# Sixteen pieces of weights on the GpSimd queue: one transformer stack on one core

## The chip, the cores and the metric

The kernel runs on one core of a Trainium2 chip. The core has a tensor engine (PE, with its weight loads listed apart as PEld), a vector engine (DVE), a scalar engine (ACT), GpSimd (POOL) and a sync engine (SP). Each runs its own instruction stream in order; they meet through semaphores. DMA transfers are issued from SP, ACT or POOL and are moved by 16 DMA engines. The metric is device time in microseconds (us), the median of the runs shown; lower is better.

## The reference

The input x has 2048 tokens of 448 features, in bf16. Four layers follow each other, each with a layer norm and a residual sum:

```
x = x + A(layernorm(x))      # layer 0
x = x + B(layernorm(x))      # layer 1
x = x + A(layernorm(x))      # layer 2, the same weights
x = x + B(layernorm(x))      # layer 3, the same weights

A: q, k, v = x @ wqkv, 16 heads of 28
   each token attends to 8 keys: itself and 2, 4, ... 14 tokens back (masked before the start)
   softmax, weighted sum of v, then @ wo (448 x 448)
B: (x @ w_gate) * (x @ w_up) @ w_down      # 448 -> 1792 -> 448, no activation
```

## The kernel before, in words

**Layout.** Even and odd tokens are split, so that a dilation of two becomes neighbouring tokens. x stays on the chip in 16 blocks of 128 tokens (`x_sb`). The layers are cut into chunks of 256 or 512 tokens; a job such as A01 is chunk 1 of layer 0, B10 chunk 0 of layer 1. `SEQ` lists the order of the jobs, so that attention chunks and GLU chunks of neighbouring layers overlap.

**Layer norm** (`ln_chunk`, lines 722 to 770). DVE computes statistics (L732, L734), ACT the reciprocal root (L735, L737), DVE the normed block `xn_sb` (L753). Blocks of layer 0 are transposed on PE against an identity (L763) and copied back by ACT or DVE (L769); later ones by a DMA transpose on SP.

**Attention.** `qk_chunk` (L823) multiplies the transposed block by WQK, accumulating over four row pieces (all matmuls of this kind have line L511, a helper). WQK is not loaded as it is: the raw rows come in four "stage" pieces into the space of `hT`, and eight copies (L675; ACT, DVE or POOL) spread each head's 28 columns over 32. Four spare columns per head carry part of V through eight more copies (L683), which wait until the first two QK chunks are done. Scores are L967, their exponential L974, the mask product L984, the weighted sum L1004, the norm L1029 to L1042, the output projection again L511, the residual sum L1059.

**GLU** (`b_chunk`, L1069). Fourteen units per chunk; each streams the chunk past gate and up weights (WGU, L511), ACT copies the gate (L1095), DVE multiplies into `hT` (L1098). The down projection WD follows (L511; for the last blocks L1110, with L1114).

**What sets the order.** A planner inside the program (`Sched`) plays all engines forward with estimated durations and landing times, and at each moment gives a free engine the ready operation with the lowest priority number. Its result is written out as fixed instruction streams. The priorities come from the job (`JP`), the kind of operation (`PR`, added by the first part of the operation's key) and the call. A transfer's key counts too: the x loads have the kind "x", so `PR['x']` moves them. The stage pieces have no entry. Estimated landings (`XL`, `STL`, `WVL`, `BL`, `WOL`) and `LINE_T`, the estimated time of a block of PE instructions, only steer the planner.

**Transfers before.** SP issues, in this order: the two halves of the first x chunk, stage pieces 1 and 3, x chunk 1, two V weight pieces, two small stage pieces, x chunks 2 and 3, four wo pieces, two WD pieces, two up pieces (L601 in the profile, the helper `plain_dma`). ACT issues stage pieces 0 and 2 first, and the two gate pieces later, held back by `tmin` (`KT`). After them SP issues the ones (L690) and the transfers that carry V (L864, L875). POOL issues none; it builds masks, constants and some copies. Before the first real matmul PE runs a fill of 96 matmuls on zeros (L666).

Of the kernel before, what the change touches and what calls it, by code (L numbers as in the profile page):

```python
# [9 lines left out]
S = 2048  # L10
D = 448
H = 16
DH = 28
F = 1792
# [3 lines left out]
NCH = S // 512  # L18
# [6 lines left out]
FC = F // 128  # L25
# [5 lines left out]
MAXALT = 2  # L31
PE_T = ("00", "01", "02", "03", "04")
HEAD_LN = 5
HEAD_P = (-381.43, -49.67, 14.22, 69.7, -45.56)
HOLD_A = 1000.0
HOLD_BA = 2000.0
HOLD_BB = 500.0
HOLD_N = 2
S_EST = 288.0
AV_EST = 288.0  # L40
# [6 lines left out]
VT = 4  # L47
# [5 lines left out]
AVC = True  # L53
AVC_E = ("act", "dve")
NBK = 8
PR = {'AV': -30.61, 'rstd': 31.29, 'bn': -4.6, 'N': -44.12, 'Gps': 146.17, 'Tps': -150.33, 'H': -24.74, 'S': 182.09, 'VT': 39.93, 'Ex': 74.94, 'G': 97.99, 'xn': -34.8, 'QK': 6.58, 'Ddps': -216.87, 'V': 10.56, 'x': -0.57, 'lnv': -319.88, 'Oc': 120.77, 'Oa': -56.11, 'R': 196.58, 'VVps': -26.27, 'Yps': -14.03, 'PW': 266.54, 'T': -7.3, 'mv': -7.38, 'Rs': 73.61, 'Rl': 145.28, 'QKps': -19.32, 'E': -12.39, 'wqk': -11.84, 'wqp': -232.02}
JP = {'A20': 55.19, 'B32': 45.24, 'B34': -59.99, 'A22': 64.41, 'B13': -156.92, 'A21': 25.01, 'B12': -69.87, 'A02': -34.56, 'A03': -34.8, 'B30': 7.81, 'B31': 37.42, 'B10': -123.7, 'B11': -163.2, 'A23': 119.73, 'A04': -39.52, 'B33': -120.76, 'A01': -46.54, 'B14': -1.29, 'A00': -55.83}
XL = (2300.0, 2200.0, 4200.0, 5000.0, 5500.0)
WVL = 5000.0
STL = (2400.0, 2600.0, 2900.0, 2800.0)  # L60
VONES_L = 18000.0
BL = (11000.0, 15000.0, 8000.0)
KT = (13000.0, 13500.0)
WOL = 6000.0
PAIR_PLAIN = (7, 7)
ACH = {0: (256, 512, 512, 512, 256), 2: (512, 512, 512, 512)}
BCH = {1: (256, 512, 512, 512, 256), 3: (256, 512, 512, 512, 256)}
# [1 line left out]
FILL = 30  # L69
SEED = 190  # L70
JITTER = 0
ATT_P = 1.96
A_CAP = 6
B_CAP = 6
SEQ = "A00 A01 B10 A02 B11 A03 A04 B12 A20 B13 A21 B14 B30 A22 B31 A23 B32 B33 B34".split()
# [58 lines left out]
class Sched:  # L134
# [8 lines left out]
    QUEUE = 64  # L143
    REFILL = 256.0
    LINE = 256
    LINE_T = 3800.0

    def __init__(self):
        self.ops = []
# [5 lines left out]
    def add(self, engs, ins, est, deps=(), prio=0.0, mode=None, acquire=None, release=(), dma=None, lat=0.0, after=None, selfd=(), tmin=None, alt=()):  # L155
        if isinstance(engs, str):
            engs = (engs,)
        if not isinstance(est, dict):
            est = {e: float(est) for e in engs}
        op = Op(engs=engs, ins=ins, est=est, deps=[d for d in deps if d is not None], mode=mode, prio=prio,  # L160
                acquire=acquire, release=release, idx=len(self.ops), dma=dma, lat=lat, after=after, selfd=set(selfd), tmin=tmin, alt=alt)
        op.deps += list(selfd)
        op.prio += JITTER * self.rng.random()
        for _, k in ins:
            k = k[0] if isinstance(k, list) and k else k
            if isinstance(k, tuple) and k[0] in PR and k[0] != "cross":
                op.prio += PR[k[0]]
                break
        self.ops.append(op)
        for n, (fn, keys) in enumerate(ins):  # L170
            for k in (keys if isinstance(keys, list) else [keys]):
                if k is not None:
                    assert k not in self.ready, k
                    self.ready[k] = (op, n)
        return op
# [364 lines left out]
def build(nc, A_x, A_wqkv, A_wo, B_w_gate, B_w_up, B_w_down, out):  # L540
# [16 lines left out]
    mv = sb([128, NBLK, 2], dt.float32, "mv")  # L557
    lnv = sb([128, NBLK], dt.float32, "lnv")
    rstd = sb([128, NBLK], dt.float32, "rstd")
# [6 lines left out]
    WGU = sb([128, 7, F], bf, "WGU")  # L566
    WD = sb([128, FC, D], bf, "WD")
# [15 lines left out]
    sc = Sched()  # L583
    LAST = sc
    sem_names = ["pe", "act", "dve", "pool"]
    sem_names += [f"d_x{i}" for i in range(NCH)] + ["d_stg0", "d_stg1", "d_stg2", "d_stg3", "d_wv", "d_wo", "d_wg0", "d_wg1", "d_wu0", "d_wu1", "d_wd0", "d_wd1", "d_out", "d_out2"]
    sem_names += ["d_x0h"]
    sem_names += [f"d_t{li}_{j}" for li in range(4) for j in range(len(CH[li]))]
    sem_names += [f"d_p{li}_{j}" for li in (0, 2) for j in range(len(CH[li]))] + [f"d_v{q}" for q in range(NQB)] + ["d_one", "d_stv"]
    vt_all = nc.dram_tensor("vt", (256, S), bf, kind="Internal").ap()  # L590
# [9 lines left out]
    def plain_dma(q, dst, src, key, sem, deps=(), lat=3000.0, prio=0.0, tmin=None):  # L600
        sc.add(q, one(lambda E: E.dma_start(dst, src), key), {"sp": 520.0, "act": 500.0, "pool": 1000.0}[q], deps=deps, dma=sem, mode=0, lat=lat, prio=prio, tmin=tmin)  # L601

    CH_ROWS = [0, 128, 192, 320]
    stage = hT[:].rearrange("p f s n -> p (f s n)")
# [10 lines left out]
        r = v.ap[0][0]  # L615
        return bass.AP(tensor=v.tensor, offset=v.offset, ap=[[r, 128], [128 * r, 2], [1, hi - lo]])

    for c in (1, 3, 0, 2):
        plain_dma("act" if c % 2 == 0 else "sp", stage[:, 2 * D * c:2 * D * (c + 1)], A_wqkv[CH_ROWS[c]:CH_ROWS[c] + 128, 0:2 * D], ("stg", c), f"d_stg{c}", lat=STL[c], prio=-60 if c % 2 == 0 else -49.9)
    load_x(1)  # L620
    for a in range(2):
        plain_dma("sp", WV[:, 2 * a:2 * a + 2, :], wv_rows(a, 2 * D, 3 * D), ("wv", a), "d_wv", lat=WVL, prio=-48.9)
# [65 lines left out]
    ones_dst = vt_all.rearrange("(t e) (a n) -> t e a n", e=32, n=128)[:, DH:32]  # L688
    ones_src = ones32[0:32, :].unsqueeze(1).to_broadcast([32, 16, 128])
    plain_dma("sp", ones_dst, ones_src, ("vones",), "d_one", deps=["c_ones"], lat=VONES_L, prio=-40)  # L690
    for j in range(4):
        dst = wo_g[32 * j:32 * j + DH, :, :]
        src = A_wo.rearrange("(c j e) d -> j e c d", c=4, j=4, e=DH)[j]
        plain_dma("sp", dst, src, ("wo", j), "d_wo", deps=["c_wo"], lat=WOL, prio=-45)
    for n in range(2):
        f0, f1 = F // 2 * n, F // 2 * (n + 1)
        plain_dma("sp", WGU[64:128, :, f0:f1], B_w_up[:, f0:f1].rearrange("(k p) f -> p k f", p=64), ("wu", n), f"d_wu{n}", lat=BL[1], prio=-43.5)
        plain_dma("act", WGU[0:64, :, f0:f1], B_w_gate[:, f0:f1].rearrange("(k p) f -> p k f", p=64), ("wg", n), f"d_wg{n}", lat=BL[0], tmin=KT[n], prio=-90)
    for n in range(2):
        plain_dma("sp", WD[:, 7 * n:7 * n + 7, :], B_w_down[F // 2 * n:F // 2 * n + F // 2, :].rearrange("(c p) e -> p c e", p=128), ("wd", n), f"d_wd{n}", lat=BL[2], prio=-44)  # L700
    WDR = [("wd", 0), ("wd", 1)]
    WO = [("wo", j) for j in range(4)]

    rings = {n: [None] * k for n, k in (("xn", NXN), ("o", NO), ("v", NV), ("v2", NV2), ("e", NE if PAIRED else 2 * NE), ("r", NR), ("g", NG))}
# [364 lines left out]
    def b_chunk(li, j, n_b, prio):  # L1069
# [4 lines left out]
        nt, b0 = t1 - t0, t0 // 128  # L1074
        tdeps = [("T", li, B) for B in range(b0, t1 // 128)]

        def unit(fc):
            acq = Banks(2, kind=1)
            def out(which):
                return ps[:, acq[which], 0:nt]  # L1080
            return dict(bk=acq, out=out, n=nt, deps=[(w, n) for w in ("wg", "wu") for n in range(2)],
                        keys=(("Gps", li, j, fc), ("Ups", li, j, fc)), fc=fc)

        us = [unit(fc) for fc in range(FC)]
        for m in range(FC):
# [6 lines left out]
            for u in us[m:m + 1]:  # L1092
                bk, fc = u["bk"], u["fc"]
                gs, prev = ring("g", ("H", li, j, fc))
                sc.add("act", one(lambda E, gs=gs, bk=bk: E.activation(g_sb[:, gs, 0:nt], ps[:, bk[0], 0:nt], ACT.Copy), ("G", li, j, fc)), act_est(nt),  # L1095
                       deps=[("Gps", li, j, fc), prev], release=[(bk, 0)], prio=prio)
                war = hslot_users.get((hs, "prev"), WQKR + [f"c_mk{k}" for k in range(3)])
                sc.add("dve", one(lambda E, gs=gs, bk=bk, fc=fc: E.tensor_tensor(hT[:, fc, hs, 0:nt], g_sb[:, gs, 0:nt], ps[:, bk[1], 0:nt], ALU.mult), ("H", li, j, fc)), dve_est(nt),  # L1098
                       deps=[("G", li, j, fc), ("Ups", li, j, fc)] + war, release=[(bk, 1)], prio=prio)
# [3 lines left out]
        for B in range(t1 // 128 - 2, t1 // 128) if last else ():  # L1103
            i = B - b0
            halves = ((0, D),) if B % 2 == 0 else ((0, D // 2), (D // 2, D))
            for c0_, c1_ in halves:
                bk = Banks(1, kind=1)
                ins = []
                for fc in range(FC):
# [5 lines left out]
                       deps=[("Dd", li, B, c0_), ("x", li - 1, B), ("xn", li, B)], release=[(bk, 0)], prio=prio)  # L1115
                r, b = divmod(B, 8)
                plain_dma("act" if c0_ == 0 and len(halves) > 1 else "sp", out_par[r][:, b, c0_:c1_], x_sb[:, B, c0_:c1_], ("out", B, c0_), "d_out2" if c0_ == 0 and len(halves) > 1 else "d_out", deps=[("x", li, B, c0_)], lat=2500.0, prio=prio)
        for i in range(0, nt // 128 - 2 * last, 2):
            B = b0 + i
            bk = Banks(2, kind=1)  # L1120
# [44 lines left out]
    for n, job in enumerate(SEQ):  # L1165
        li, j = int(job[1]), int(job[2])
        prio = (-20.0 if job[0] == "A" else 0.0) + n * 0.5 + JP.get(job, 0.0)
        if n == 0:
# [72 lines left out]
```

## Time and profile before

| | |
|---|---|
| median of 3 runs | 395.79 us (395.49 to 396.33) |
| profiled execution, span from first to last instruction | 394.6 us |
| first QK matmul in the profile | 9.67 us |
| first matmul that reads WGU | 60.2 us |
| PE busy | 382.7 us (97%) |
| DVE, ACT, POOL busy | 279.5, 200.8, 8.0 us |
| moved by DMA | 22.52 MB |

The profile is one execution recorded by the hardware; its own time is given as the span, and the median of the runs lies 1.2 us above it. The page lists busy time per engine, a timeline in 40 slices, the DMA queues, the chain of work that ended last, and the costliest groups of instructions. Arrows name outputs and inputs (`ps<-xnTa,WQK`). "idle" is the time an engine stood just before an instruction, with what ended it; "issue" there means that nothing which the profile shows was being waited for. The granted clock is the share of full speed that PE was given.

### The profile page before, as it was taken

To read this page: it belongs to the slowest core of one execution; us is meant where nothing else is said; L and a number is where in the kernel's file an instruction comes from. 1 tells how busy PE (TensorE), PEld (TensorE's weight loads), DVE (VectorE), ACT (ScalarE), POOL (GpSimd) and SP (SyncE) were. 2 spreads that over 40 slices of the span, in tenths; PEclk is the share of its full clock that TensorE was granted. 3 is DMA by queue.
4 is the path that set the end of the run, shared out by engine and by line. 5 is a ranking of instruction groups with operands and counts; after the bars stand their busy time and mean duration, and the time that the engine had idled before them with its cause. 6 is when DMAs were issued, how large, how long until landed. Compare 5 with 4: busy or idle time off the path is not lost.

```text
span 394.6 us, 14517 instructions
## 1 busy us (share of the span) xinstructions
PE 382.7 (97%) x6452; PEld 215.6 (55%) x6452; DVE 279.5 (71%) x604; ACT 200.8 (51%) x390; POOL 8.0 (2%) x36
## 2 busy tenths in 40 slices
PE   7878999999999999999999999999999999999996
PEld 5535558755455544445455777754455544444584
DVE  6886999999896766753665888889674884723152
ACT  4684788867742546731234647564582563421040
POOL 7000000000000000000000000000000000000000
PEclk9998999999999999999999999999999999999999
DMA  8990043245102410002433104312300060021000
GB/s 273 310 302 8 5 60 59 39 53 94 29 10 44 94 20 17 2 10 40 82 46 42 27 22 46 62 40 48 64 16 27 25 94 2 2 47 48 25 26 25
DMA packets 54706, 22.52 MB, mean 57 GB/s; under 512 B 44836, under 2 KB 54644, under 8 KB 54644
## 3 DMA queue, kind: packets, MB, share of 16 engines
q1 hardware_dynamic: 53284, 19.47, 24.4%
q10 hardware_dynamic: 1360, 2.12, 1.6%
q8 instruction: 51, 0.84, 0.9%
q14 instruction: 11, 0.09, 0.1%
HBM read 8.54 MB, written 2.71 MB: 29 GB/s over the span
## 4 chain that ended last, share of the span: by engine, by line
PE 88%; DVE 4%; ACT 2%; DMA 2%; issue 2%; SPq 1%; DVEq 0%
PE ps L511 80%; PE ps L967 3%; PE ps L1004 2%; DMA x_sb<-in_A_x_dram 2%; PE ps L514 2%; PE ps L1110 1%; SPq L601 1%; ACT E_sb L974 1%; DVE R_sb L1029 1%; ACT R_sb L1030 1%; DVE st L732 1%; DVE O_sb L1015 0%; DVE oT L1042 0%; DVE hT L1098 0%; DVE xn_sb L753 0%
## 5 line engine op out<-in xcount | busy, mean ns | idle before, releaser
L511 PE MATMUL ps<-xnTb,WGU 64*128 64x512 bf16 (+1 forms) x1926 | 174.5, 333 | 0.2
L511 PEld LDWEIGHTS ps<-xnTb,WGU 64*128 64x128 bf16 x1926 | 93.3, 94 | 70.9 <-DVE x_sb L1059 0.7
L1095 ACT ACTIVATE g_sb<-ps 128x512 bf16<-128x512 f32 (+1 forms) x140 | 71.5, 512 | 93.0 <-PE ps L511 86.9
L1098 DVE TENSOR_TENSOR hT<-g_sb,ps 128x512 bf16<-128x512 bf16 (+1 forms) x140 | 79.4, 574 | 38.5 <-ACT g_sb L1095 36.6
L511 PE MATMUL ps<-WD,hT 64*128 64x448 bf16 x828 | 81.1, 349 | 0.0
L1059 DVE TENSOR_TENSOR x_sb<-x_sb,ps 128x448 bf16<-128x448 bf16 x62 | 36.2, 614 | 35.2 <-PE ps L511 35.2
L511 PEld LDWEIGHTS ps<-WD,hT 64*128 64x128 bf16 x828 | 39.8, 94 | 37.3 <-issue 0.3
L511 PE MATMUL ps<-xnTa,WQK 64*128 64x512 bf16 (+1 forms) x500 | 54.4, 361 | 4.5 <-issue 3.3
L732 DVE BATCH_NORM_STATS2 st<-x_sb 128x6 f32<-128x448 bf16 x64 | 37.7, 611 | 3.6 <-DMA x_sb<-in_A_x_dram 3.4
L511 PEld LDWEIGHTS ps<-xnTa,WQK 64*128 64x128 bf16 x500 | 23.8, 97 | 27.4 <-issue 4.2
L974 ACT ACTIVATE E_sb<-ps 128x1024 bf16<-128x1024 f32 (+1 forms) x36 | 33.9, 979 | 8.2 <-PE ps L967 7.9
L753 DVE TENSOR_SCALAR xn_sb<-x_sb,mv,rstd 128x512 bf16<-128x512 bf16 (+1 forms) x64 | 34.3, 572 | 1.0 <-PE ps L763 1.0
L855 ACT ACTIVATE qk<-ps 128x1024 bf16<-128x1024 f32 (+1 forms) x20 | 18.8, 939 | 18.0 <-PE ps L511 17.8
L511 PE MATMUL ps<-wo_g,oT 64*128 64x448 bf16 x240 | 27.6, 350 | 0.2
L984 DVE TENSOR_TENSOR E_sb<-E_sb,MK 128x1024 bf16<-128x1024 bf16 (+2 forms) x40 | 23.9, 610 | 4.0 <-ACT E_sb L974 3.7
L855 DVE CAST qk<-ps 128x1024 bf16<-128x1024 f32 (+1 forms) x16 | 17.4, 1088 | 13.0 <-PE ps L511 13.0
L735 ACT ACTIVATE lnv<-mv,eps_sb 128x2 f32<-128x2 f32 (+1 forms) x33 | 9.5, 294 | 32.1 <-DVE mv L734 31.7
L1030 ACT ACTIVATE R_sb<-R_sb 128x480 f32<-128x480 f32 (+1 forms) x34 | 20.4, 607 | 9.8 <-DVE R_sb L1029 9.7
L1042 DVE TENSOR_TENSOR oT<-O_sb,R_sb 128x480 bf16<-128x480 f32 (+3 forms) x36 | 22.2, 627 | 4.4 <-ACT R_sb L1031 4.2
L511 PE MATMUL ps<-WV,xnTa 64*128 64x336 bf16 (+3 forms) x252 | 23.1, 304 | 0.5 <-ACT xnTa L769 0.5
L1029 DVE STREAM_SHUFFLE R_sb<-O_sb 128x480 f32<-128x480 f32 (+1 forms) x34 | 23.0, 692 | 0.1
L1031 ACT ACTIVATE R_sb<-R_sb 128x480 f32<-128x480 f32 (+1 forms) x34 | 20.3, 608 | 0.5
(57 smaller groups left out, 199.8 us busy)
## 6 DMA issues: line engine op xcount, KB each, us to landing
out_dram<-x_sb SPq DMA_DIRECT2D x15, 112.0 KB, 1.7
WD<-in_B_w_down_dram SPq DMA_DIRECT2D x2, 784.0 KB, 8.4
WGU<-in_B_w_up_dram SPq DMA_DIRECT2D x2, 784.0 KB, 15.2
WGU<-in_B_w_gate_dram ACTq DMA_DIRECT2D x2, 784.0 KB, 13.2
x_sb<-in_A_x_dram SPq DMA_DIRECT2D x3, 448.0 KB, 5.5
vt<-qk SPq DMA_DIRECT2D x42, 16.0 KB
xnTb<-xn_sb SPq DMA_TRANSPOSE x32, 3.0
x_sb<-in_A_x_dram SPq DMA_DIRECT2D x2, 224.0 KB, 4.1
```

The source lines that it names most:

```text
L511: return lambda E: E.matmul(out(), lhs(), rhs(), start=start, stop=stop)
L732: sc.add("dve", one(lambda E, B=B: E.bn_stats(st6[:, B, :], x_sb[:, B, :]), ("bn", li, B)), 525.0, deps=[("x", li - 1, B)] + ([("xn", li - ...
L753: sc.add("dve", one(lambda E, B=B, dst=dst, src=src: E.tensor_scalar(dst, src, mv[:, B, 0:1], rstd[:, B:B + 1], ALU.subtract, ALU.mult), ( ...
L855: return E.activation(dst, src, ACT.Copy) if hasattr(E, "activation") else E.tensor_copy(dst, src)
L974: return E.activation(E_sb[:, slot, 2 * hp:2 * hp + 2, 0:w], ps[:, b0:b0 + 2, 0:w], ACT.Exp, scale=SCALE)
L984: return E.tensor_tensor(e, e, m, ALU.mult)
L1029: sc.add("dve", one(lambda E: E.stream_shuffle(R_sb[:, rs, 0:w], O_sb[:, os_, 0:w], [DH] * 32), ("Rs", li, qb)), dve_est(w) + 100.0, deps= ...
L1030: sc.add("act", one(lambda E: E.activation(R_sb[:, rs, 0:w], R_sb[:, rs, 0:w], ACT.Ln), ("Rl", li, qb)), act_est(w, False), deps=[("Rs", l ...
L1042: return E.tensor_tensor(oT[:, :, a % HALF:a % HALF + z - a], O[:, :, a - tok:z - tok], R_sb[:, rs, 0:w].rearrange("p (h n) -> p h n", h=4 ...
L1059: sc.add("dve", one(lambda E: E.tensor_tensor(x_sb[:, B, :], x_sb[:, B, :], ps[:, bk[w], 0:D], ALU.add), ("x", li, B)), dve_est(D), deps=[ ...
L1095: sc.add("act", one(lambda E, gs=gs, bk=bk: E.activation(g_sb[:, gs, 0:nt], ps[:, bk[0], 0:nt], ACT.Copy), ("G", li, j, fc)), act_est(nt), ...
L1098: sc.add("dve", one(lambda E, gs=gs, bk=bk, fc=fc: E.tensor_tensor(hT[:, fc, hs, 0:nt], g_sb[:, gs, 0:nt], ps[:, bk[1], 0:nt], ALU.mult), ...
```

## The change

Stage piece 0, 2 and 3 are issued on ACT, piece 1 stays on SP. The wo, gate, up and down weights, formerly 10 transfers on SP and ACT, become 16 (four of wo, eight of gate and up, cut by rows into 4 and 3 of 7 row groups, four of down), all issued on POOL. The first two wait until the last x chunk has landed, each later one for the landing of the piece two in front; each has its own semaphore. A GLU unit of the first half of the columns waits only for that half's pieces. The priorities, hold times and estimated landings of the planner get new values, so the order on every engine is new. One consequence can be read from the new order: on SP all five x transfers now stand first, then stage piece 1, then the V weights. On PE, 72 rows of the merged listing stand ahead of the first GLU matmul, as before, with one more burst of scores and one more of weighted sums among them.

```diff
-HEAD_P = (-381.43, -49.67, 14.22, 69.7, -45.56)
-HOLD_A = 1000.0
-HOLD_BA = 2000.0
-HOLD_BB = 500.0
+HEAD_P = (-4486.73, -2491.14, -1697.23, 2169.7, -4568.26)
+HOLD_A = 2037.8
+HOLD_BA = 5494.4
+HOLD_BB = 8266.9
...
-PR = {'AV': -30.61, ..., 'x': -0.57, ...}
+PR = {'AV': -2347.39, ..., 'x': -4264.98, ...}
-JP = {'A20': 55.19, ...}
+JP = {'A20': -3293.36, ...}
...
+KP = ((0, 4), (4, 7))
+BULK_Q = "pool"
+BULK_DEPTH = 2
+BULK_AFTER = [("x", -1, 15)]
...
-    LINE_T = 3800.0
+    LINE_T = 2900.0
...
-    for c in (1, 3, 0, 2):
-        plain_dma("act" if c % 2 == 0 else "sp", stage[...], A_wqkv[...], ("stg", c), f"d_stg{c}", lat=STL[c], prio=-60 if c % 2 == 0 else -49.9)
+    for c in (1, 0, 2, 3):
+        plain_dma("sp" if c == 1 else "act", stage[...], A_wqkv[...], ("stg", c), f"d_stg{c}", lat=STL[c], prio=-49.99 if c == 1 else -60)
...
+    chain = []
+
+    def bulk(dst, src, key, sem, lat):
+        prev = chain[-BULK_DEPTH] if len(chain) >= BULK_DEPTH else None
+        plain_dma(BULK_Q, dst, src, key, sem, deps=([prev] if prev else []) + ["c_wo"] + BULK_AFTER, lat=lat, prio=-50.0 + len(chain) * 0.1)
+        chain.append(key)
+
     for j in range(4):
...
-        plain_dma("sp", dst, src, ("wo", j), "d_wo", deps=["c_wo"], lat=WOL, prio=-45)
+        bulk(dst, src, ("wo", j), f"d_wo{j}", WOL)
     for n in range(2):
         f0, f1 = F // 2 * n, F // 2 * (n + 1)
-        plain_dma("sp", WGU[64:128, :, f0:f1], B_w_up[...], ("wu", n), f"d_wu{n}", lat=BL[1], prio=-43.5)
-        plain_dma("act", WGU[0:64, :, f0:f1], B_w_gate[...], ("wg", n), f"d_wg{n}", lat=BL[0], tmin=KT[n], prio=-90)
-    for n in range(2):
-        plain_dma("sp", WD[:, 7 * n:7 * n + 7, :], B_w_down[...], ("wd", n), f"d_wd{n}", lat=BL[2], prio=-44)
-    WDR = [("wd", 0), ("wd", 1)]
+        for m, (a, z) in enumerate(KP):
+            for w, W_ in enumerate((B_w_gate, B_w_up)):
+                bulk(WGU[64 * w:64 * w + 64, a:z, f0:f1], W_[64 * a:64 * z, f0:f1].rearrange("(k p) f -> p k f", p=64), (("wg", "wu")[w], n, m), f"d_w{'gu'[w]}{n}{m}", BL[0])
+    for n in range(4):
+        f0, f1 = (0, 4, 7, 11, 14)[n:n + 2]
+        bulk(WD[:, f0:f1, :], B_w_down[...], ("wd", n), f"d_wd{n}", BL[2])
+    WDR = [("wd", n) for n in range(4)]
...
-            return dict(..., deps=[(w, n) for w in ("wg", "wu") for n in range(2)], ...)
+            return dict(..., deps=[(w, n, m) for w in ("wg", "wu") for n in range(1 + (fc >= FC // 2)) for m in range(len(KP))], ...)
```

## The prediction

> **What bounds the kernel now.** I read the page's busy table first, then busy time by stage, then what the tensor engine (PE) waited for, then the chain, then the transfers.
>
> ```profile
> PE 382.7 (97%) x6452; PEld 215.6 (55%) x6452; DVE 279.5 (71%) x604; ACT 200.8 (51%) x390; POOL 8.0 (2%) x36
> PEclk9998999999999999999999999999999999999999
> ```
> PE is the bound: 382.7 of 394.6 us. What can be won is in the 12 us in which it stood, and in the one stage with a lower clock digit.
>
> ```profile
> 9.66:32.00 22.34, 16.99 (x376) 10.09 (x378) 17.38 (x50) 15.40 (x35) 0.73 (x4) 1.00 0.90 274
> 32.00:60.20 28.20, 27.41 (x684) 15.76 (x680) 24.90 (x51) 19.58 (x33) 0.00 (x0) 0.94 0.19 26
> 60.20:394.60 334.40, 330.69 (x5284) 184.07 (x5284) 231.17 (x487) 160.96 (x312) 0.00 (x0) 1.00 0.22 39
> 32.00:35.50 3.50, 3.44 (x36) 2.22 (x33) 2.62 (x5) 1.01 (x3) 0.00 (x0) 0.52 0.02 5
> ```
> Busy time by stage (length, then PE, weight load, DVE, ACT, POOL; clock, DMA share, GB/s). 9.66 us is the first real matmul, 60.2 the first one that reads the GLU weights. PE stood 5.35 us in the first stage and 0.8 in the second; after 60.2 it stood 3.7, of which 3.3 fall after 380. The last line: for some 3.4 us the granted clock was half.
>
> ```profile
> PE ps L511 <- issue: 3.3, 2, 2.3
> PE ps L967 <- DVE qk L855: 1.0, 1, 1.0
> PE ps L511 <- DVE WQK L683: 0.8, 1, 0.8
> ```
> PE's own waits between 9 and 60 us (total, times, longest). The largest is "issue": nothing in the program was awaited.
>
> ```profile
> 22.28 0.99 issue
> ...
> 28.60 2.32 issue
> ```
> The chain puts those two at 22.28 and 28.60. The records of queue 8 explain them: it carries 51 blocks of 16 KB, one per 256 of PE's instructions. One block started at 28.55, just as the bulk weights had drained, took 0.99 us, and PE resumed at 30.92. The block before started at 20.68, 4 to 6 us after PE had entered the stretch that asks for it. With the queues empty, PE resumed at 30.91 and the next block started at 32.02. So a refill costs 1.1 to ask, 1.0 to move, 1.4 to resume: 3.5 us, plus up to 5.3 us behind bulk data. The half clock (32.1 to 35.5) follows that stall and costs 3.4 x 0.5 = 1.7 us.
>
> ```profile
> GB/s 0 0 62 310 386 392 389 376 379 357 321 377 381 309 208 199 294 343 340 338 334 300 348 385 369 371 346 371 377 324 310 228 129 31 6 0 19 0 0 0
> ```
> ```profile
> x_sb<-in_A_x_dram SPq DMA_DIRECT2D x1, 448.0 KB, 5.4
> WV<-in_A_wqkv_dram SPq DMA_DIRECT2D x1, 224.0 KB, 5.5
> ```
> Transfers from 0 to 35 us (slices of 0.875 us) and two landings. Summing the slices: 1.84 MB by 7.4 us, 2.29 by 8.7, 2.75 by 10.0. The second x chunk is the fifth transfer on SP; what stands ahead of it, itself and ACT's share are 1.84 MB, and it landed at 2.8 + 5.4 = 8.2: its bytes' time plus 0.75. The landings keep the order of issue.
>
> **The change, part by part.**
>
> **1. Stage weights.** Read by its own order, the change issues stage pieces 0, 2, 3 on ACT, but piece 1 stays on SP and now stands behind all five x transfers (the new x priority, -4265, lifts x past it). All four pieces are needed for the first QK matmul. Ahead of piece 1 and with it: x 1.84 + ACT's 0.69 + 0.23 = 2.75 MB, by 10.0 us, so landed at 10.75 (it was 1.8 + 4.4 = 6.2). Engines run in order: behind that wait stand, on DVE, the xn of the second block and everything after it; on ACT, the copies of both transposed blocks. DVE: weight copy 0.24, xn 0.41, to 11.4; transposes 0.28. ACT: weight copy 0.56, first copy 0.60, lnv 0.29, second copy 0.60: 12.85. First QK at 12.85 against 9.67: **+3.2**. Bounds: +2.2 (queues a fifth faster) to +4.0. The extra ACT issue (0.46) lies at 1.8 us, where ACT idles until 5.74.
>
> **2. PE's clock at the start.** The warm-up fill (82+12+2 matmuls, as many as before) ends near 9.0, so PE stands some 3.4 of 3.85 us. In the row above, 2.3 us of standing was followed by 3.4 us at half clock: up to +1.7. But DVE, held 2.4 us by piece 1, delivers the blocks for the two-block transposes only near 21.3 (its row durations added up), about 1.0 after PE could take them: **+1.0**, which hides part of the slow clock: **+0.5** (0 to 1.7).
>
> **3. x earlier.** The last x chunk lands near 10, not 14.5. DVE's 0.97 us wait and PE's 1.05 behind it go: **-1.05**. The 0.8 on the padding copies stays: they still wait for the second chunk's QK.
>
> **4. Bulk.** SP loses nine issues (some 8 us of its time to 15.06); nobody waits for SP there. ACT loses two (1.36 at 14.1, in an idle stretch). POOL gains 16, each held by a landing. Behind them on POOL stand two mask sums and three padding copies. Masks: the first two weight pieces follow x, so they come near 13, needed after 27. Copies: they are reached near 18 but wait for PE until 27, and that holds the chain: ten pieces are queued behind them. From 27.5 on, three rounds of two finish gate/up. A round is one landing: no POOL transfer is in the trace; nearest rows 3.4 us (224 KB) and 9.6 us (784 KB, loaded); I take 5 for pieces of 344 to 458 KB. Gate/up land at 43 (38 to 56), first read near 64; down weights at 53, read near 72. Cost **0**: the cover is 46.6 us of QK, V and attention matmuls ahead of the first GLU one (42.9 before); gone if a round exceeds 12 us.
>
> **5. Code blocks.** The two old stalls go: **-3.3**, and the half clock **-1.7**. Dividing the new order into 256 instructions, most stretches hold 5 to 7 us of matmuls; three hold 3.1, 3.5 and 3.4 us (near 27, 44 and 48 us), in which bulk is in flight, at most two pieces: 0.92 MB at 0.385 MB/us, 2.4 us. Refill 3.5 to 5.9: stalls 0.4 to 7.7 in all; with half the wait 1.5 + 0.7 + 0.5 = **+2.7**, and **+0.3** for a chance of the slow clock.
> The Trainium skill, "Runtime: NRT & Kernel Launch", Instruction fetch mechanics, says that crossing a 16 KiB boundary is mostly hidden; the trace differs (2.32 us). By the page the +2.7 would be 0 and the sum 394.2.
>
> **6. The rest of the head**: copies awaited 0.6 go, 0.5 come: **-0.1**.
>
> **7. New order after the head.** The old one stands 0.5 us from 60 to 380, so there is nothing to win. The matmuls are the same; bursts of attention are 18 and 18. DVE's row durations summed between one hT product and the next, less PE's matmuls between the same GLU units, pile up to 5.4 us at most (7.2 in the old order, which PE did not feel). **+0.5** (-0.5 to +3). At the end 28 down-projection matmuls now stand between the last GLU unit and the final ones, covering the 0.93 us wait for the last hT: **-0.9**.
>
> Sum: 3.2 + 1.0 + 0.5 - 1.05 - 3.3 - 1.7 + 2.7 + 0.3 - 0.1 + 0.5 - 0.9 = +1.15. The profiled span, 394.6, becomes 395.75; the runs' median lies 1.2 above the span, so **396.9**.
>
> **The rivals.**
> *Code arrives in time* (other side). With little in flight refills take 3.5 us: stalls 0.4 in all, no slow clock anywhere: 396.9 - 2.3 - 0.8 = 393.8. For: queue 8 waited little whenever DMA was idle. It decides if the three stalls stay under 1.5 us. If piece 1 also comes early (some engines run ahead), 390.6.
> *Code behind bulk.* Each short stretch meets two full pieces: 7.7 instead of 2.7, with one more slow clock (1.4): 401-403. For: the 5.3 us wait at 23.3. Against: a sixth of the data in flight.
> *POOL starves.* DVE is busy 9.15 of 10 us from 40 to 50; if POOL can only write its transfers in DVE's gaps, a 5 us round grows to 15, gate/up land at 72, and PE stands 8 us: 405. Against: POOL's copies beside a busy DVE took 0.56 and 0.69 us.
> The Trainium skill, "SBUF — State Buffer", on the trap in which VectorE blocks a GpSimd DMA, speaks for this last one: it gives 620 ns alone and 3100 overlapped. No run here shows it yet.
> *The new order stands.* Units whose DVE lag meets a full ring cost 2 to 4 us: 399.5.
>
> **How the numbers follow.** Forecast 0.42 (395.6 to 398.6); code in time 0.28, with early piece 1 0.04; code behind bulk 0.10; new order stands 0.10; POOL starves 0.06. A measurement tells some 0.2% (0.8 us). Faster: 0.25 + 0.04 + 0.02 of the forecast = 0.31. Within: 0.03 + 0.10 = 0.13. Slower: 0.56. The range 392.8 to 400.8 leaves out the last rival, half of code behind bulk and the 390.6.
>
> **What would show it.** First QK matmul near 12.85 (not 9.7) and DVE waiting for stage weights from 8.2; x landed by 10; clock near 0.5 somewhere in 12 to 17; first GLU matmul near 65; "issue" waits near 30, 44 and 48 totalling 1 to 4 us; no wait of PE on a weight transfer; no wait ahead of the final matmuls. The prediction is wrong if piece 1 lands before 8, if PE waits for WGU, or if PE stands over 3 us between 65 and 380.

## The result, and the profile after

The changed kernel takes 394.64 us (median of 20 runs, 393.78 to 396.83). The kernel before, run beside it, takes 396.84. The ratio is 0.9942, with a 95% interval of 0.9926 to 0.9958: **faster by 0.6%**, some 2.3 us, where +1.15 us was forecast. The time lies inside the range given, on the wrong side of the kernel before. All ratios leave out executions over 1.5% above the fastest of their kernel: one of the kernel before here (653.57 us), and below two of the six of depth1 (the medians keep them).

The profiled execution happens to be the longest of the 20 (396.83 us, span 394.8). The others have spans of 391.8 to 394.0. The busy table, and the granted clock by slices of 9.87 us:

```profile
PE 384.4 (97%) x6428; PEld 218.7 (55%) x6428; DVE 276.5 (70%) x607; ACT 204.3 (52%) x387; POOL 19.1 (5%) x52
PEclk9699989999999999999999999999999999999999
```

PE is still the bound. The clock now has its low digits in the second slice and, less so, in the sixth, where before it was in the fourth. Busy time by stage, in the columns used before (length, PE, weight load, DVE, ACT, POOL; clock, DMA share, GB/s):

```profile
9.66:32.00 22.34, 19.44 (x394) 12.51 (x396) 17.95 (x58) 17.29 (x40) 6.87 (x15) 0.85 0.46 114
32.00:60.20 28.20, 26.61 (x650) 14.82 (x652) 23.22 (x51) 22.77 (x34) 5.55 (x8) 0.94 0.57 138
60.20:380.00 319.80, 319.04 (x5142) 177.26 (x5140) 225.59 (x476) 158.60 (x302) 0.00 (x0) 1.00 0.23 40
...
10.67:17.50 6.83, 5.76 (x72) 4.07 (x74) 5.61 (x18) 4.10 (x11) 4.17 (x9) 0.50 0.45 119
48.22:51.63 3.41, 3.41 (x29) 1.48 (x22) 1.66 (x3) 3.27 (x5) 1.01 (x2) 0.50 0.74 219
```

PE stood 2.9 us in the first of these stages (5.35 before) and 1.6 in the second (0.8). But the last two rows have a granted clock of 0.50, and if "busy" is worth half there, the two stretches cost up to 2.9 and 1.7 us (estimates: half of their PE time). From 9.66 to 32 the DMA moves 114 GB/s instead of 274, and from 32 to 60.2 it moves 138 instead of 26: the bulk has been spread out. What PE waited for between 9 and 60 us (total, times, longest):

```profile
PE ps L776 <- DVE xn_sb L766: 2.4, 1, 2.4
PE ps L980 <- issue: 1.3, 1, 1.3
PE ps L515 <- POOL WQK L687: 0.6, 1, 0.6
```

The two issue waits of 3.3 us have become one of 1.3. The first line is new: DVE had to wait for a stage piece, and PE for DVE. The chain says the same:

```profile
3.67 6.87 DMA hT<-in_A_wqkv_dram
...
12.35 2.87 PE ps L515 x26
...
46.38 1.29 issue
```

Stage piece 1 landed at 10.54, and the first QK matmul came at 12.35 instead of 9.67. The gate, up and down pieces landed in 3.5 to 6.3 us each, the small wo pieces in 2.6 to 3.3. Two rows (KB, median us from issue to landing):

```profile
WGU<-in_B_w_gate_dram POOLq DMA_DIRECT2D x2, 448.0 KB, 4.8
WGU<-in_B_w_up_dram POOLq DMA_DIRECT2D x2, 448.0 KB, 6.2
```

Gate and up were complete at 46.06, the down weights at 54.9, and the first GLU matmul came at 66.24: PE waited for no weight of the bulk. So a loss at the start came as forecast, and yet the kernel is faster. The experiments look for what pays for it.

### The profile page after: what moved, and what is told of

Same layout as the page of the kernel before. It is cut to its first block, busy times and chain, and to the rows that moved or that the text cites. A ratio compares the mean times of both kernels' runs of the same rounds, so it can differ in the third digit from the quotient of the medians.

```text
span 394.8 us, 14494 instructions
## 1 busy us (share of the span) xinstructions
PE 384.4 (97%) x6428; PEld 218.7 (55%) x6428; DVE 276.5 (70%) x607; ACT 204.3 (52%) x387; POOL 19.1 (5%) x52
## 4 chain that ended last, share of the span: by engine, by line
PE 84%; DVE 7%; DMA 3%; ACT 3%; issue 1%; SPq 1%; POOL 0%; DVEq 0%
PE ps L515 77%; PE ps L980 2%; PE ps L1017 2%; DMA hT<-in_A_wqkv_dram 2%; PE ps L1123 1%; PE ps L518 1%; DVE xn_sb L766 1%; DVE x_sb L1072 1%; DMA xnTb<-xn_sb 1%; DVE R_sb L1042 1%; DVE st L745 1%; ACT E_sb L987 1%; DVE hT L1111 1%; SPq L605 1%; DVE O_sb L1028 1%
## 5 line engine op out<-in xcount | busy, mean ns | idle before, releaser
L515 PE MATMUL ps<-WD,hT 64*128 64x448 bf16 x832 | 83.5, 349 | 0.0
L868 ACT ACTIVATE qk<-ps 128x1024 bf16<-128x1024 f32 (+1 forms) x29 | 26.9, 937 | 12.3 <-PE ps L515 11.8
L515 PE MATMUL ps<-wo_g,oT 64*128 64x448 bf16 x244 | 28.7, 357 | 0.0
L515 PE MATMUL ps<-WV,xnTa 64*128 64x336 bf16 (+3 forms) x252 | 25.0, 318 | 0.0
L1028 ACT ACTIVATE O_sb<-ps 128x512 f32<-128x512 f32 (+2 forms) x20 | 11.3, 576 | 13.7 <-PE ps L1017 13.7
```

The source lines that it names most:

```text
L515: return lambda E: E.matmul(out(), lhs(), rhs(), start=start, stop=stop)
L868: return E.activation(dst, src, ACT.Copy) if hasattr(E, "activation") else E.tensor_copy(dst, src)
```

## The experiments

All kernels compute everything. They leave the planner alone: its order is taken as it stands, and the entries named are moved, replaced or freed of their waits before it is written out, so that nothing else in the order shifts. `take_out(queue, semaphores)` removes the transfers with those semaphores from a queue's order, and `place(queue, position, entries)` puts them back elsewhere. Times are medians; each group of four was run beside the kernel before, which had 397.44, 396.88 and 397.38 us in the three groups. Ratios are to it, with 95% intervals; they are estimated apart, so they differ a little from the quotient of two medians. The changed kernel itself was not run again in these groups, so differences of medians between groups carry the 0.5 us by which the kernel before moved.

| kernel | order of matmuls | start loads | bulk | us | ratio |
|---|---|---|---|---|---|
| changed | new | as changed | two in flight | 394.64 | 0.9942 (0.9926 to 0.9958) |
| early_piece | new | piece 1 early | two in flight | 394.12 | 0.9916 (0.9883 to 0.9949) |
| unpaced | new | as changed | all at once | 400.79 | 1.009 (1.0065 to 1.0114) |
| late_piece | old | as changed | as before | 401.37 | 1.011 (1.0082 to 1.0139) |
| paced_bulk | old | as before | two in flight | 390.97 | 0.9857 (0.9822 to 0.9891) |
| old_loads | new | as before | two in flight | 395.02 | 0.9955 (0.9932 to 0.9979) |
| warm_fill | new | as changed | two in flight | 395.41 | 0.9959 (0.9938 to 0.9981) |
| depth4 | old | as before | four in flight | 395.49 | 0.9969 (0.9945 to 0.9993) |
| depth1 | old | as before | one in flight | 407.53 | 1.0227 (1.0185 to 1.0269) |
| mixed_loads | new | fitted to it | two in flight | 390.92 | 0.9837 (0.9813 to 0.9861) |
| warm_fill2 | new | as changed | two in flight | 393.36 | 0.9902 (0.988 to 0.9924) |
| unpaced_old | old | as before | all at once | 398.77 | 1.0035 (1.0013 to 1.0058) |
| order_alone | new | as before | as before | 399.91 | 1.0058 (1.0031 to 1.0085) |

### The bulk alone, in the old order: paced_bulk

The order is that of the kernel before; its ten bulk transfers are taken off SP and ACT, and the sixteen pieces of the change put on POOL, six ahead of the padding copies and ten behind.

```diff
     sc.schedule()
+    take_out("sp", *old)
+    take_out("act", *old)
...
+        op = sc.add("pool", one(lambda E: E.dma_start(dst, src), key), 1000.0, deps=([prev] if prev else []) + ["c_wo", ("x", -1, 15)], dma=sem, mode=0)
...
+    place("pool", at_op("pool", "c_mk2") + 1, ents[:6])
+    sc.order["pool"] += ents[6:]
```

> The kernel before with only the bulk weights as the change has them: 16 pieces on POOL behind the last x chunk, each on the landing of the piece two in front, six ahead of POOL's padding copies and ten behind; the rest of the order as before. Theory 1: the two issue waits (0.99 and 2.32) and the half clock behind them (1.7) go, 396.8 - 3.3 to 5.0 = 391.8 to 393.5, the late x chunk also comes no later. Rival (the code blocks stall as they did, since the old order meets the same short stretches): 396 to 397.2. If the new order is what gained, this one stays at 396 to 397.2 as well, but with the waits gone.

Measured: 390.97 us, 6.5 below the kernel before by the medians (5.7 by the ratio), more than theory 1 expected. PE's two longest waits between 13 and 62 us, and its busy time from 20 to 46; the last row is the kernel before:

```profile
PE ps L511 <- DVE xnTa L769: 0.9, 1, 0.9
PE ps L511 <- ACT lnv L735: 0.6, 1, 0.6
```
```profile
20.00:32.00 12.00, 11.03 (x370) 7.27 (x370) 11.13 (x32) 9.89 (x19) 4.24 (x11) 1.00 0.69 153
32.00:46.00 14.00, 13.36 (x286) 7.13 (x282) 12.97 (x27) 11.38 (x20) 3.69 (x6) 1.00 0.68 173
```
```profile
20.00:32.00 12.00, 7.83 (x202) 4.07 (x200) 8.29 (x24) 8.87 (x18) 0.73 (x4) 1.00 0.73 241
```

The issue waits are gone but for one of 0.2 us at 74 us, and the clock is 1.00 in both rows; five of the six executions have a mean clock of 1.000. From 20 to 32 PE is busy 11.03 us; before it was 7.83. The wait for the last x chunk went as well: with no bulk beside it, it landed at 13.40 instead of 14.49. So the bulk alone gains more than the whole change, and something in the rest of the change gives some 3.5 us back (3.7 by the medians, 3.4 by the ratios).

### Is it the pace, or the queue and the small pieces? unpaced, unpaced_old, depth4, depth1

The changed kernel with its chain of landings cut (unpaced), and the same sixteen pieces, all at once, in the old order (unpaced_old):

```diff
     sc.schedule()
+    for op in sc.ops:
+        if op.dma and op.eng == "pool":
+            op.deps = ["c_wo"] + BULK_AFTER
+    rest = [e for e in sc.order["pool"] if e[0][0].dma and e[0][0].dma not in ("d_wo0", "d_wo1")]
+    take_out("pool", *[e[0][0].dma for e in rest])
+    place("pool", at_op("pool", "c_mk2") + 1, rest)
```

> The changed kernel with the landings between the bulk pieces taken away: the 16 pieces are issued one behind the other on POOL as soon as the last x chunk has landed, ahead of the three padding copies instead of ten of them behind; no other order moves. Theory 1 (the landings between the pieces keep the code blocks' way free, and this is where the gain came from): PE's issue waits return to 2 to 4 us in 20 to 50 us, with one more stretch of half clock (1.7): 394.6 + 2 to 5 = 396.6 to 399.6. Rival (the new order of the matmuls gained, the bulk's pace did not): 394.0 to 395.2, issue waits as before at most 1.3.

> The kernel before with the bulk weights in the same 16 pieces on POOL behind the last x chunk, but none waiting for another, all 16 ahead of POOL's padding copies. It differs from the paced bulk (0.986) in the pace, and from the kernel before in queue and piece size. Theory 1 (only the pace gains): 0.997 to 1.012, two or three issue waits of 1 to 4.5 us between 20 and 40 us. Rival (small pieces on POOL's queue gain by themselves): 0.985 to 0.992.

Measured: 400.79 and 398.77, both slower than the kernel before; unpaced is slower than its theory 1 allowed (396.6 to 399.6). PE's longest waits between 13 and 62 us, first in unpaced, then in unpaced_old:

```profile
PE ps L980 <- issue: 4.5, 1, 4.5
PE ps L776 <- issue: 1.2, 1, 1.2
```
```profile
PE ps L511 <- issue: 2.6, 1, 2.6
PE ps L1004 <- issue: 1.9, 1, 1.9
```

The issue waits are back, 5.7 and 4.5 us of them. POOL's queue and the small pieces gain nothing by themselves; the pace does: in the changed kernel it is worth 5.9 us by the ratios (1.009 against 0.9942), in the old order 7.1 (1.0035 against 0.9857). POOL's padding copies are not the reason: they ran at 23.66 in unpaced_old and at 23.32 in paced_bulk. The next two kernels are paced_bulk with another number of pieces in flight (`DEPTH` 4 and 1 instead of 2).

> Paced bulk in the old order, with four pieces in flight instead of two (each piece on the landing of the piece four in front). Theory 1 (what counts is how many bytes stand ahead of a code block): up to 1.7 MB, 4 us, ahead of a block, so that issue waits of 1 to 3 us return: 0.988 to 0.996 of the kernel before, against 0.986 with two. Rival (any pacing will do): 0.983 to 0.988, and no issue wait over 0.5 us.

> Paced bulk in the old order, with one piece in flight. Theory 1: code blocks meet at most one piece and wait no more than with two; two left 0.2 us of issue waits, so nothing more is to be won there. Ten pieces are issued after the padding copies at some 24 us, each a round of 3.5 to 4.5 us: gate and up land at 45 to 51 and the down weights at 59 to 69; the first GLU matmul came at 55 to 56 with two. Ratio 0.983 to 0.988 if the weights are still in time; rival (a round is 5 us or more): PE waits for WGU or WD, 0.988 to 0.996.

Measured: 395.49 with four (a ratio of 0.9969, just above theory 1), 407.53 with one (402.88 to 412.87; its trace is of the longest of the six executions). With four, PE's longest waits were

```profile
PE ps L1004 <- issue: 2.8, 1, 2.8
PE ps L763 <- issue: 2.2, 1, 2.2
```

So "any pacing will do" is wrong: what stands ahead of a code block counts. The trace lets one measure it. In calm stretches a block of code starts to move near the moment when PE reaches instruction 256k - 66, where weight loads and matmuls are counted and the 66 is fitted: blocks 3 to 8 of paced_bulk start between 0.1 us before that moment and 0.8 us after it. Counting PE's instructions in each trace gives the lateness of block k against that moment; the table has the two latest that started between 12 and 62 us, and all issue waits of PE in that span:

| kernel | latest two blocks, us | issue waits, us |
|---|---|---|
| late_piece (below) | 7.55, 4.22 | 3.9 |
| before | 6.05, 5.06 | 3.3 |
| unpaced | 5.48, 5.45 | 5.7 |
| unpaced_old | 5.14, 4.69 | 4.5 |
| order_alone | 5.08, 4.11 | 3.8 |
| depth4 | 4.40, 4.23 | 5.4 |
| changed | 3.01, 2.75 | 1.3 |
| mixed_loads (below) | 3.07, 2.37 | 1.6 |
| paced_bulk | 2.80, 0.75 | 0 |

Kernels with blocks 4 us late or more lose 3 to 6 us of PE's time in issue waits; those whose blocks are up to 3.1 us late lose 0 to 1.6. The lateness grows with the bulk data in other queues: the latest block is 2.8 to 3.1 us late with two pieces in flight, 4.4 with four, 5.1 to 7.6 with all. PE is stopped about 256 instructions after the moment of asking, if the block has not come by then: in the kernel before, the block asked for at 23.5 started at 28.55, and PE stood from 28.60, at the instructions where the next one would have been asked for.

With one piece in flight the program fails in another place, which neither theory had. PE's longest wait, and POOL's stream (start, duration; the idle time before, and what ended it):

```profile
PE ps L511 <- POOL WQK L683: 10.1, 1, 10.1
```
```profile
27.44 0.64 POOL L1201 DMA_DIRECT2D WGU<-in_B_w_gate_dram  x1 [2.23 <-DMA wo_g<-in_A_wo_dram]
32.32 0.63 POOL L1201 DMA_DIRECT2D WGU<-in_B_w_up_dram  x1 [4.24 <-DMA WGU<-in_B_w_gate_dram]
32.94 0.73 POOL L683 COPY WQK<-hT 128x64 bf16<-128x64 bf16 x4
```

The padding copies stand behind six pieces on POOL, each of which waits for a landing. They ran at 32.94 instead of 23.32, and PE stood 10.1 us for them. A wait on a queue's engine is a wait for all that stands behind it there. The rival came as well: the last up piece landed at 69.5, the last down piece at 91.4, and PE waited ahead of the first GLU matmul at 71.48 and again at 91.54:

```profile
PE ps L511 <- DMA xnTb<-xn_sb: 5.4, 1, 5.4
PE ps L1004 <- DMA WD<-in_B_w_down_dram: 2.3, 1, 2.3
```

### The start: late_piece, early_piece, old_loads, mixed_loads

The old order and bulk, with the start loads of the change:

```diff
     sc.schedule()
+    place("act", 3, take_out("sp", "d_stg3"))
+    xs = take_out("sp", "d_x1", "d_x2", "d_x3")
+    place("sp", 2, xs)
+    s1 = take_out("sp", "d_stg1")
+    place("sp", 5, s1)
```

> The kernel before with only the loads of the start as the change has them: on SP all five x transfers and then stage piece 1, and piece 3 on ACT behind 0 and 2; bulk, and the order of all else, as before. Step 1 says +2.7 to +3.2 with x earlier -1.05: 396.8 + 1.7 to 2.2 = 398.5 to 399. If PE's half clock follows the wait, up to 400. Rival (hidden by DVE's later lag): 395.8 to 397.

Measured: 401.37, that is +3.9, more than either expected. Besides a wait of 3.8 us on DVE there were stretches of half clock from 12.14 to 15.55 and from 29.21 to 32.62, and 4.7 us of issue waits in the whole run (3.3 before). The delay also moved the gate pieces on ACT from 14.1 to 18.7 us, so they stood in the queue for longer. So the new start loads do cost, in the old order, but not all of the 3.9 is the wait itself. In the new order, piece 1 was put back to its early place:

```diff
     sc.schedule()
+    place("sp", 2, take_out("sp", "d_stg1"))
```

> The changed kernel with one entry moved: stage piece 1 goes back on SP to the place behind the two halves of the first x chunk, as in the kernel before; nothing else moves. The first QK matmul came at 12.35 us after the change and at 9.67 before. Theory 1 (the late piece costs what step 1 says, and the gain came from the code blocks and from elsewhere): first QK near 9.7, no wait of 2.4 us of PE ahead of the second transposes, time 394.6 - 2.7 = 391.9 us (391 to 392.8), and down to 390.5 if the half clock of 10.7 to 17.5 goes with it. Rival (the late piece costs nothing, because DVE with 23 weight copies, xn and statistics in its way hands over the later blocks no sooner): 394 to 394.8.

Measured: 394.12, ratio 0.9916 against 0.9942, with overlapping intervals. The first QK matmul came at 9.18, so the piece was in time; and yet hardly anything was won. Theory 1 (391 to 392.8) was wrong; the rival had the number, but not the reason that the trace shows. PE's longest wait between 9 and 20 us:

```profile
PE ps L515 <- DMA WV<-in_A_wqkv_dram: 2.7, 1, 2.7
```

The wait of 2.4 us has become one of 2.7, further down the queue: the V weights stand behind x as well. A stretch of half clock followed it, from 14.52 to 17.93. So the next run put all start loads back as they were before.

```diff
     sc.schedule()
+    place("sp", 2, take_out("sp", "d_stg1") + take_out("act", "d_stg3"))
+    mid = take_out("sp", "d_wv", "d_stv")
+    i = next(i for i, e in enumerate(sc.order["sp"]) if e[0][0].dma == "d_x1")
+    place("sp", i + 1, mid)
```

> The changed kernel with all its start loads issued in the order of the kernel before (x first chunk, stage pieces 1 and 3, second x chunk, V weights, the other two x chunks, all on SP); the paced bulk on POOL and the new order of the matmuls stay. With piece 1 alone put back, the wait of 2.4 us became one of 2.7 us on the V weights, which then stood behind x as well. Theory 1 (the whole set of start loads costs 3.9 us, as it did in the old order, paced bulk pays 6.5, and the new order of the matmuls some 0.2 at most): time like that of the paced bulk in the old order, 0.984 of the kernel before (0.982 to 0.988), no wait of PE on V weights, first QK near 9.7. Rival (the new order was made for the late piece and cannot use it early): 0.990 to 0.995, with another wait of 2 to 3 us ahead of 20 us.

Measured: 395.02, ratio 0.9955: no gain at all. Theory 1 was wrong again, and the rival came nearly as put (0.990 to 0.995, with another wait). The wait had moved a second time:

```profile
PE ps L776 <- DVE xn_sb L766: 2.7, 1, 2.7
DVE st L745 <- DMA x_sb<-in_A_x_dram: 3.0, 1, 3.0
```

DVE itself waited 3.0 us for the last x chunk, which landed at 13.46. In the new order DVE asks for the statistics of the last chunk after those of six blocks; in the old order (paced_bulk) after nine. This suggested a second theory: the new order needs stage piece 1, the V weights and the last x chunk, all by about 10.5 us, and does not yet need the third chunk.

```diff
     sc.schedule()
+    place("sp", 2, take_out("sp", "d_stg1"))
+    x2 = take_out("sp", "d_x2")
+    i = next(i for i, e in enumerate(sc.order["sp"]) if e[0][0].dma == "d_stv")
+    place("sp", i, x2)
```

> The changed kernel with its SP loads as the new order of the matmuls asks for them: x first chunk, stage piece 1, second x chunk, last x chunk, V weights, and only then the third x chunk. In the new order each load order tried so far left one wait of 2.4 to 3.0 us: piece 1 (as changed), V weights (piece 1 early), the last x chunk at 13.4 us (old loads). By the bytes in front, the last x chunk lands at 9.5 to 10.2 here and the V weights at 10.7 to 11.2, both needed near 10.5, the third chunk near 11.9. Theory 2 (new order and loads belong together: it needs piece 1, V weights and the last chunk by 10.5, and only the wait costs): the wait shrinks below 0.8 us, ratio to the kernel before 0.984 to 0.989. Rival (the head has slack, DVE is late anyway, and the first QK matmul does not set the time): 0.992 to 0.996 whatever lands when.

Measured: 390.92, ratio 0.9837. The last chunk landed at 9.42, the V weights at 10.76, the third chunk at 12.01. PE's longest wait between 9 and 20 us, and its busy time from 9.66 to 20:

```profile
PE ps L515 <- ACT xnTa L782: 0.6, 1, 0.6
```
```profile
9.66:20.00 10.34, 10.28 (x200) 6.73 (x202) 10.30 (x33) 8.48 (x23) 5.09 (x10) 1.00 0.58 156
```

PE is busy 10.28 of 10.34 us, at full clock. One x chunk of 448 KB issued behind the V weights, and the stage piece back in front, are worth 3.7 us against the changed kernel (4.2 by the ratios). With loads that fit it, the new order takes 390.92, and the old order with its own loads and the same bulk 390.97: no gain of the new order is seen. Both are faster than the kernel before and the changed one.

The new order without any of the rest, order_alone (bulk in ten unpaced pieces on SP and ACT, start loads as before):

> The new order of the matmuls alone: the changed kernel with the start loads of the kernel before on SP and ACT, and the bulk as before too, in 10 unpaced pieces at their old places on SP and ACT. With paced bulk and old loads the new order had 0.9955 and the old order 0.986, so it costs 0.010 there. If parts add up: 1.010 (1.006 to 1.014), with the 2.7 us wait on the last x chunk and the old issue waits. Rival (the old issue waits and the wait on x overlap): 1.000 to 1.006.

Measured: 399.91, ratio 1.0058, at the edge between the two. The waits are of both kinds, on code as in the kernel before and on the x chunk as in old_loads:

```profile
PE ps L980 <- issue: 3.4, 1, 3.4
PE ps L776 <- DVE xn_sb L766: 3.0, 1, 3.0
```

From it to old_loads only the bulk differs: 4.1 us by the ratios (1.0058 to 0.9955). In the old order the bulk was worth 5.7 by the ratio.

### What the slow clock costs: warm_fill, warm_fill2

PE stands for 2.4 us ahead of the second block's transposes, and the clock is half from 10.67 to 17.50. The two runs put warm-up matmuls (2.1 us at full clock by the expectation, 2.32 in warm_fill2) into that, with the number of instructions unchanged. In the first, warm_fill, the fill stands one entry too late, behind the transposes. `first` are the warm-up pairs 0 to 19, each made 512 columns wide; the place `i` is that of warm-up pair 47 in warm_fill, and that of the transposes (`Tps`, 0, 1) in warm_fill2.

```diff
     sc.schedule()
...
+    late = first[1::2]
+    sc.order["pe"] = [e for e in sc.order["pe"] if e not in late]
...
+    sc.order["pe"][i:i] = late
```

> The changed kernel with PE kept at work while it waits for stage piece 1: the first 20 pairs of warm-up matmuls become 10 pairs of twice the columns, and the 10 pairs saved, of twice the columns too, stand ahead of the last warm-up pair, 2.1 us at full clock. The number of instructions is the same, so the code blocks fall where they fell. Theory 1 (the 2.4 us of standing bring one or two stretches of half clock in 10.7 to 17.5): clock 1.0 through 20 us, a gain of 1 to 3 us, ratio to the kernel before 0.985 to 0.991 where the change itself has 0.994. Rival (the slow clock lies beside waits for DVE, and costs nothing): 0.993 to 0.995.

> The fill of the run before it, in the place meant for it: 10 pairs of warm-up matmuls of twice the columns (2.1 us) stand ahead of the second block's transposes, so PE works through the wait for stage piece 1; in that run they stood behind the transposes, kept the first QK matmul to 14.93 instead of 12.35, and cost only 0.8 us. Theory 1 (the slow clock costs): half clock gone from 10 to 18 us, ratio 0.985 to 0.991. Rival (2.6 us of delay cost 0.8, so there is slack of 1.8 us here, and a slow clock in it costs no more than the same): 0.992 to 0.995.

Measured: 395.41 and 393.36. The misplaced fill is a test of its own; PE's stream in warm_fill (start, duration):

```profile
11.16 0.40 PE L776 MATMUL ps<-ident,xn_sb 64*128 64x64 bf16 x8 [2.76 <-DVE xn_sb L766]
11.36 3.62 PE L1200 MATMUL ps<-hT 64*128 64x512 bf16 x20
14.82 0.27 PE L670 MATMUL ps<-hT 64*128 64x256 bf16 x2
14.93 1.25 PE L515 MATMUL ps<-xnTa,WQK 64*128 64x256 bf16 x20
```

It kept the first QK matmul to 14.93, 2.6 us after that of the changed kernel, and cost 0.8. Part of the delay was paid back by the clock: the trace has one stretch of half clock (3.41 us) instead of two at the start, and 5 of 12 executions have a mean clock of 1.000 instead of 2 of 20. But those five take 394.37 (median), only 1.0 more than warm_fill2, where the first QK matmul comes at 12.34. So less than half of a delay of the first QK matmul reaches the end, and something later sets part of the pace; that it is the blocks that DVE hands over later is likely, but not shown. In its right place the fill keeps the clock at 1.00:

```profile
9.66:20.00 10.34, 8.99 (x168) 5.95 (x166) 9.40 (x30) 7.93 (x23) 5.04 (x10) 1.00 0.54 146
```

All six executions have a mean clock of 1.000, and 1.3 us are gained (394.64 to 393.36; 1.6 by the ratios). It is the price of the slow clock at the start, if nothing else in the fill helps; that stays open, for the two executions of the changed kernel with a mean clock of 1.000 took 394.18 and 394.19, only 0.5 below its median. From there to mixed_loads, where the wait itself is gone, it is another 2.4 us (2.6 by the ratios), about the length of the wait.

## Why the prediction was wrong

The forecast was +1.15 us, and the measurement some -2.3. The step that failed is **step 5**, the code blocks: the mechanism was right, and the term for the new stalls was put at 2.7 and measured 1.3. Step 2 failed too, by less, and the kernel from which the sum starts was taken some 1 us too fast.

- **Step 1 (late stage piece, +3.2).** Right in mechanism: landed 10.54 (10.75 forecast), first QK 12.35 (12.85), DVE waiting 2.6 us from 7.96. It was put at 3.2; taking away the wait and those behind it gave 2.4 (mixed_loads against warm_fill2; 2.6 by the ratios).
- **Step 2 (half clock +0.5, late DVE +1.0).** Put at 0.5, the slow clock costs 0.5 to 1.3 (the changed kernel's executions without it, and warm_fill2). The late transposes cost nothing that shows: in warm_fill2, at full clock and with the same late piece, PE has no wait over 0.2 us between the first QK matmul at 12.34 and 26.2 us. The start was put at 4.7 and costs 3.7, by what mixed_loads gains. The prediction did not see that moving the piece alone wouldn't end the wait: behind it stand the V weights, and behind those the last x chunk.
- **Step 3 (x earlier, -1.05).** x landed at 9.95 and the wait went. But paced_bulk shows that bulk leaving x's neighbourhood removes it too.
- **Step 4 (bulk on POOL costs 0).** Right: gate and up at 46.06 (43 forecast, bounds 38 to 56), POOL held by its padding copies until 28.3, PE at no time waiting for bulk weights.
- **Step 5 (-3.3 - 1.7 + 2.7 + 0.3 = -2.0).** The old stalls and the slow clock behind them went, as said: paced_bulk has 0.2 us of issue waits and full clock. The new stalls were put at 2.7 with half the longest wait behind two pieces; they measured 1.3, and 1.6 in mixed_loads. The step's own arithmetic does not give 2.7: with half the wait, a refill of 4.7 less stretches of 3.1, 3.5 and 3.4 is 1.6 + 1.2 + 1.3 = 4.1, so worked out as stated it would have missed by more. The clock's share was put at 0.3; 16 of the 20 executions of the changed kernel have at most one stretch of half clock (mean clock 0.996 or 1.000), presumably the one at the start. The rule of the step held; its inputs were off. It says that a stall is the block's lateness, 1.0 to move and 1.4 to resume, less the length of the stretch. Half the wait means a lateness of 2.3 in each of the three short stretches (1.1 to ask and half of 2.4 in the queue); it was 1.01 in that from 27.35, 2.42 in that from 42.6, and 1.58 in that from 47.7. The first, 3.47 long, thus had to hold 1.01 + 0.92 + 1.4 = 3.3 and did not stall. The second had to hold 2.42 + 1.19 + 1.4 = 5.0 and was 3.8 long without its stall: 1.2 by the rule, 1.29 measured. The third had to hold 4.0, and the slow clock had drawn it out to 5.1 in this execution.
- **Step 7 (+0.5 and -0.9).** The wait ahead of the final matmuls went, as said, and in mixed_loads PE has no wait over 0.2 us between 62 and 380 us, so the +0.5 did not come. That the two orders still come out equal (390.92 against 390.97) fits the 1.6 us of issue waits in the new one, against 0.2 in the old one and the 0.9 that it stands ahead of its final matmuls.

Summed up: without the start, the forecast was 1.15 - 4.7 = -3.55. Measured, mixed_loads is 6.5 below the kernel before. Of the 2.9 between them, 1.1 are the new stalls (2.7 put, 1.6 there), 0.3 the clock put beside them, and 0.5 the order after the head. The last 1.0 is about the error of the base: the sum was made against one execution and a median of three runs (395.79), and the kernel before has 396.84 over 20. Its time differs from one execution to the next (394.5 to 398.5 in the first group), while mixed_loads keeps within 390.6 to 391.2; that its issue waits make the difference is likely, but only argued. The start gives another 1.0 (4.7 put, 3.7 measured). Together 3.9, where 3.4 is wanted; the 0.5 between them is how far the kernel before moved from group to group.

What happened is the rival "Code arrives in time", put at 393.8 with a chance of 0.28, with its own condition met: the three stalls stayed under 1.5 us. Its number is in part luck, for it put the stalls at 0.4 and had no slow clock anywhere, while the trace has 1.3 and 18 of 20 executions have a mean clock below 1. The evidence on which it was set below the forecast, one block 5.3 us late, came from a stretch with all bulk queued and said little of a stretch with two pieces queued. The Trainium skill, "Runtime: NRT & Kernel Launch", Instruction fetch mechanics, says that crossing a 16 KiB boundary is mostly hidden. With two pieces in flight the runs nearly agree (issue waits of 0.2 us in paced_bulk, 1.3 and 1.6 in the new order); with four or all they disagree (5.4 and 5.7). The forecast set that rule aside because of a stall under other conditions.

Two things stay open. No kernel run had the change's loads and the paced bulk in the old order, so the loads' price there is known only beside unpaced bulk (+3.9, with 1.4 us more of issue waits in it). And the wait at 46.38 was not taken away by itself, so that it ends with a block of code is read from the times of the blocks alone.

## What to carry to other kernels

Bulk weights that are needed late shouldn't stand in the queues all at once: the tensor engine's own code comes by DMA too, and here pacing them on POOL alone was worth 5.7 to 6.5 us of 397, with two pieces in flight; four gave most of it back, and one made other work wait. When a wait at the start is taken away, look what the engines ask for next and when it lands; here three load orders gave nearly the same wait on three different transfers, and of those tried only an order of loads made from the order of use gave a clear gain. And a wait put on an engine's own stream holds all that stands behind it there (10.1 us for four small copies).

## What the runs showed of the hardware

- Standing for 2.4 to 2.7 us at the start was followed by half clock in most executions: 18 of 20 of the changed kernel, 5 of 6 of early_piece, and 9 of 11 of old_loads had a mean clock below 1, and so had 7 of 12 of warm_fill, with 2.8 us. With no wait over 0.9 us between 9 and 60 us: none of 10 in mixed_loads and warm_fill2, and 1 of 6 in paced_bulk. Such a wait does not always slow the clock: the traced execution of depth4 stood 2.8 and 2.2 us and kept 1.00. The stretches in the profiles, but for those cut off by the end, last 3.41, 6.83 or 10.24 us.
- A block of code comes later the more data other queues hold: it was up to 7.6 us late with all bulk queued on SP and ACT, 5.5 with all on POOL, 4.4 with four pieces of 336 to 448 KB in flight, 3.1 or less with two.
- POOL issues a transfer in 0.59 to 0.81 us (all 16 of the changed kernel); the eight from 32 to 60 us take 0.61 to 0.79 while DVE is busy 82% of that time. The Trainium skill, "SBUF — State Buffer", A bandwidth-pool intuition that's wrong (but worth ruling out), gives 620 ns for a GpSimd DMA alone and 3100 beside a VectorE copy that holds the port they share; the rows show the former and not the latter. The rival built on it, "POOL starves", didn't come.
